# Eight of sixteen row gathers issued two experts ahead, and their two tiles turned inside the choice of width

## The chip, the cores and the metric

One core of a Trainium2 chip runs the kernel. The metric is device time in microseconds (us), the median of several executions. A profile is one further execution, recorded instruction by instruction; its times are counted from the first instruction. PE is the matrix engine (TensorE), DVE is VectorE, ACT is ScalarE, POOL is GpSimd and SP is SyncE, which issues the weight loads.

## The reference

A windowed attention (each query sees the first 8 keys and its last 96) over 4 batches of 8 heads, 768 positions and 64 dimensions makes 3072 rows x of 512 numbers. A router then sends each row to one of 8 experts:

```python
xn = x / (norm(x) + 1e-6);  en = expert_emb / (norm(expert_emb) + 1e-6)
logits = xn @ en.T / tau
expert_idx = argmax(logits, axis=1);  gate_w = softmax(logits)[expert_idx]
for e in range(8):
    mask = expert_idx == e
    h = maximum(x[mask] @ w1[e], 0)                      # 512 -> 1024
    out[mask] = gate_w[mask, None] * (h @ w2[e])         # 1024 -> 512
```

## The kernel before

The first 190 us are the attention and the routing; they leave x in DRAM (`x_dram`) and, for each expert, the list of its rows. From then on a Python loop, unrolled, treats experts 0 to 7 one after another. The change is in that loop, from expert 1 on. All engines run their instructions in the order in which the program lists them.

**PE, for expert e.** First comes the *choice of width*: a switch with nine arms, one for each count of rows from 256 to 512 in steps of 32. In the chosen arm `first_by_seven` (L1331) makes the hidden values with seven products instead of eight, sixteen matmuls each (L1347). After a product DVE adds what it left in PSUM to an earlier one (L1357), and the fourth product can write its bank only when DVE has read the second product out of it. The arm then makes the second matrix product for rows beyond 256 (L1281, L1294). Behind the switch stands the *pair* (class `Pair`, L1153 to L1227), the seven products for the first 256 rows. Its last product writes a bank that ACT reads first (L1206), and ACT gets to that only behind an instruction that needs a sum made by DVE (u3, L1189).

**DVE, for expert e.** In the arm: the additions, and at fixed places (`spare`, a list with one entry per place; the first place, ahead of the first product, is empty) the sums of weights. Behind the switch, for e of 2 and more: it ends the pair of expert e-1, then turns the four tiles of gathered rows of expert e+1 (`turn_squares`, L1036 to L1042, four `STREAM_TRANSPOSE`s at L1039), then adds the pair's u2, then makes four sums of the turned rows (L1090 to L1093), then u3.

**POOL, for expert e** (called *stage e* below). `prepare(e + 1)` issues the sixteen gathers of expert e+1 (`gather_quarters`, L1030): four tiles of 128 rows, each in four quarters of 64 KB. From the fifth gather on, before every second one, a small copy (L1029) reads a value that an earlier gather brought, so POOL waits there until the two gathers issued four and three places earlier have landed. Then come the six scatters of finished rows (L1300), and a `drain` (L1795). POOL then goes on to stage e+1. For expert 2 the loop issues four gathers in `prepare` and twelve behind the scatters.

**SP.** The weights of expert e+1 (w1 2 MB, then w2 2 MB) are loaded in place of those of expert e-1: w1 when expert e-1's pair has begun, w2 when it has ended.

The gathered tiles come from a pool of eight buffers, two experts' worth. x after turning has two buffers.

Of the kernel before, what the change touches and what calls it, by code (L numbers as in the profile page):

```python
# [9 lines left out]
F32 = mybir.dt.float32  # L10
# [10 lines left out]
P = 128  # L21
NEG = 1e9
CAP = 512
# [998 lines left out]
def gather_quarters(k, ids, xgs, lo, hi):  # L1022

    src = k.x_dram[:, :].rearrange("t (b c) -> (t b) c", b=4)
    for i in range(lo, hi):
        j, g = divmod(i, 4)
        if g % 2 == 0 and i - lo > 3:
            m, h = divmod(i - 4, 4)
            k.nc.gpsimd.tensor_copy(out=k.landed[0:1, 0:2], in_=xgs[m][0:1, h * P : (h + 2) * P : P])  # L1029
        k.nc.gpsimd.indirect_dma_start(  # L1030
            out=xgs[j][:, g * P : (g + 1) * P], out_offset=None, in_=src,
            in_offset=bass.IndirectOffsetOnAxis(ap=ids[:, j, g : g + 1], axis=0),
        )


def turn_squares(k, xgs, xT, j):  # L1036

    half = P // 2
    k.nc.vector.transpose(  # L1039
        out=xT[:, :, :, j * half : (j + 1) * half].rearrange("p c a (g i) -> p g c a i", i=LACE),  # L1040
        in_=xgs[j][:].rearrange("p (g r c) -> p g c r", g=4, r=SQ),
    )  # L1042
# [345 lines left out]
def expert(k, now, coming, widths, unfinished):  # L1388
# [15 lines left out]
    more, ahead, turns = [], [], []  # L1404
    if coming:
        coming.token_sums, more = token_sums(k, coming.xT)
        if now.e:
            coming.first_sums, ahead = first_sums(k, coming.w[0])
            turns = [lambda j=j: turn_squares(k, coming.rows[2], coming.xT, j) for j in range(CAP // P)]
    spare = [[], spare[:2], spare[2:3], spare[3:], ahead[:1], ahead[1:2]]  # L1410
    tiles = range(2 if now.e else 1, CAP // P)
    ps = None if now.e else k.work0.tile([P, k.DM], F32, name="work", tag="work")
    k.order = list(range(4, 8)) + list(range(4)) if now.e else list(range(8))
# [24 lines left out]
    def choose_next():  # L1438
        if coming:
            give_hint(k, coming.e, widths[coming.e])  # L1440

    out = [scatters]
    if now.e:
        pair = Pair(k, now.rows, a, left, w2, now.sums, not coming)
        choose_next()
        out += unfinished.pop()()
        number = [lambda: widths.append(take_width(k, now.e + 2))] if now.e + 2 < k.E else []
        if now.e == k.E - 2:
            number.append(lambda: load_flag(k))
        if now.e == 2:  # L1450
            ahead.append(lambda: flag_leftover(k))
        if now.e > 1:
            for make in turns:
                make()
        pair.begin(spare=(more, number, ahead[2:]) if now.e > 1 else ([], number, turns + more + ahead[2:]))
        ps = k.work0.tile([P, k.DM], F32, name="work", tag="work")
        unfinished.append(pair.end(ps[:, 0:256]))
        out.append(pair.scatter(1))
    else:
        choose_next()  # L1460
        widths.append(take_width(k, 2))
        out += unfinished.pop()()
        for make in more:
            make()
        second(k, ps, hT, w2, range(k.NF // 2, k.NF))
        unfinished.append(lambda: end_second(k, now.rows, ps))
# [83 lines left out]
def take_width(k, e):  # L1550

    t = Net()
    n = len(widths_of(e))
    engines = ARMS if e else ARMS[:2]
    v = k.nc.values_load(k.pick[0:1, e : e + 1], engines=engines, min_val=0, max_val=n - 1)
    t.index, t.hint = {eng: v for eng in engines}, "expert%d" % e
    return t
# [22 lines left out]
def load_flag(k):  # L1580
    k.any = k.nc.values_load(k.fi[0:1, 1:2], min_val=0, max_val=1)
# [58 lines left out]
def kernel(  # L1640
# [13 lines left out]
    n = Net()  # L1654
# [26 lines left out]
    with ExitStack() as moe:  # L1681
# [40 lines left out]
        def cast(lo, hi):  # L1722
            nc.vector.tensor_copy(out=n.ids[:, lo:hi], in_=n.mt[:, lo:hi, :, 0:2])

        def prepare(e):
            t = Net()
            t.e = e
            t.y, t.y_part = ys[e % 2]
            if e < 2:
                xgs, t.gathers = gather_rows(n, n.ids[:, e], n.xgp)  # L1730
            else:
                xgs = [n.xgp.tile([P, n.DM], F32, name="xg", tag="xg") for _ in range(CAP // P)]
                gather_quarters(n, n.squares[:, e], xgs, 0, 4 if e == 2 else 16)
            t.rows = n.mt[:, e], n.ids[:, e], xgs
            if e < 2:
                t.w = n.w[e]
            else:
                t.w = new_weights(n, (wp_a, n.wp_b)[e % 2])
            return t

        with tc.manual_schedule(engines=ORDERED | set(ARMS) | {mybir.EngineType.Pool}):
# [38 lines left out]
            for e in range(n.E):  # L1780
                now, coming = coming, None
                parts_of(n, now)
                now.width = widths[e]
                if e == 1:
                    now.first_sums = first
                if e + 1 < n.E:
                    coming = prepare(e + 1)
                for scatter in pending:
                    scatter()
                if e == 1:  # L1790
                    gather_quarters(n, n.squares[:, 2], coming.rows[2], 4, 16)
                if e and coming:
                    wait_for(n, load_weights(n, e + 1, coming.w), [n.outs[-1] if e == 1 else n.out_again])

                nc.gpsimd.drain()  # L1795
                pending = expert(n, now, coming, widths, unfinished)
# [33 lines left out]
```

## Time and profile before

| | |
|---|---|
| median of 3 executions | 515.23 us (513.41 to 517.9) |
| the profiled execution | 510.97 us |
| its span, first to last instruction | 509.2 us |
| mean granted clock of TensorE | 0.999 |
| busy: PE, DVE, ACT, POOL | 95%, 64%, 36%, 48% of the span |

The span leaves 1.8 us of the profiled execution outside it. A busy share is an average over the attention and the experts. "Idle before" in a row is the time that the engine did nothing before that instruction, and the name after the arrow is what ended it; "issue" means that the profile shows nothing it waited for.

### The profile page before, as it was taken

How to read it: one execution, taken by the hardware profiler on the slowest of the kernel's cores; microseconds unless marked ns; L12 is line 12 of the kernel's file. 1: busy time of each engine (PE TensorE's matmuls, PEld its weight loads, DVE VectorE, ACT ScalarE, POOL GpSimd, SP SyncE). 2: the span in 40 equal slices, each digit the busy share in tenths (PEclk: the TensorE clock that was granted, in tenths of full speed). 3: DMA queues.
4: the chain of work that ended last, by engine and by line, in shares of the span. 5: the costliest groups of instructions: out<-in, count | busy, mean ns of one | idle time of the engine just before them, and what ended most of it. 6: DMA issues, size and time to landing. Idle time of an engine off the chain costs nothing.

```text
span 509.2 us, 13692 instructions
## 1 busy us (share of the span) xinstructions
PE 484.6 (95%) x5510; PEld 399.1 (78%) x5510; DVE 325.3 (64%) x642; ACT 183.2 (36%) x445; POOL 243.7 (48%) x275
## 2 busy tenths in 40 slices
PE   7999999999999898999899999999979989999995
PEld 7677787787877687879788479789869679859964
DVE  5656677666777665848467745777656764744631
ACT  4967767858665311302112121222112111312210
POOL 4221131251453426477568575826855856854022
PEclk9999999999999999999999999999999999999999
DMA  9989999998542627529661156265354274112001
GB/s 169 195 187 189 216 240 221 201 222 208 159 106 70 180 48 179 180 79 343 203 200 41 53 200 202 75 223 181 108 188 173 54 258 163 43 70 81 0 23 68
DMA packets 112864, 76.35 MB, mean 150 GB/s; under 512 B 88517, under 2 KB 96709, under 8 KB 112721
## 3 DMA queue, kind: packets, MB, share of 16 engines
q1 hardware_dynamic: 103057, 59.00, 44.3%
q0 software_dynamic: 8064, 15.27, 9.6%
q8 instruction: 63, 1.03, 0.9%
q14 instruction: 80, 0.66, 0.4%
q10 hardware_dynamic: 1600, 0.39, 0.3%
HBM read 61.66 MB, written 17.16 MB: 155 GB/s over the span
## 4 chain that ended last, share of the span: by engine, by line
PE 71%; issue 8%; DMA 6%; POOL 6%; DVE 5%; ACT 4%; POOLq 0%; DVEq 0%; ACTq 0%
PE big L1347 22%; PE big L1153 9%; PE od L514 7%; PE work L1281 7%; PE pa L485 5%; PE pa L460 3%; DMA xg<-x_dram,squares 3%; PE work L1153 3%; PE od L524 3%; PE pa L683 2%; POOL out_dram L1300 2%; ACT ex L491 2%; PE big L1324 2%; POOL xg L1030 2%; PE work L1294 1%
## 5 line engine op out<-in xcount | busy, mean ns | idle before, releaser
L1030 POOL DMA_INDIRECT xg<-x_dram,squares x96 | 105.0, 1093 | 57.2 <-issue 42.6
L498 DVE TENSOR_TENSOR ex<-ex,table 126x768 f32<-126x768 f32 x64 | 60.7, 953 | 37.0 <-ACT ex L491 36.8
L1357 DVE TENSOR_TENSOR hT<-big,hT 128x320 f32<-128x320 f32 (+4 forms) x70 | 39.4, 565 | 56.3 <-PE big L1347 55.8
L1347 PE MATMUL big<-xT,w1t 128*128 128x160 f32 (+4 forms) x336 | 59.4, 330 | 1.6 <-issue 1.6
L491 ACT ACTIVATE ex<-pa 126x384 f32<-126x384 f32 (+1 forms) x128 | 53.2, 479 | 16.6 <-PE pa L485 15.8
L1347 PEld LDWEIGHTS big<-xT,w1t 128*128 128x128 f32 x336 | 54.8, 190 | 4.5 <-issue 2.5
L261 POOL DMA_INDIRECT meta<-mt,slot x24 | 28.5, 1187 | 41.3 <-DVE rd L558 18.2
L514 PE MATMUL od<-ex,v 126*64 126x192 f32 (+1 forms) x576 | 46.0, 305 | 0.0
L1359 ACT ACTIVATE hT<-hT 128x320 f32<-128x320 f32 (+4 forms) x42 | 22.3, 531 | 56.6 <-DVE hT L1357 56.6
L514 PEld LDWEIGHTS od<-ex,v 126*64 126x64 f32 x576 | 34.7, 136 | 7.5 <-issue 3.7
L435 POOL COPY v<-v 30x896 f32<-30x896 f32 (+1 forms) x15 | 17.2, 1158 | 47.8 <-DMA v<-in_v_dram 31.5
L1347 PE MATMUL big<-xsum,fsum 128*128 128x160 f32 (+4 forms) x224 | 39.6, 330 | 0.0
L485 PE MATMUL pa<-qT,kT 64*32 64x128 f32 (+3 forms) x2048 | 37.6, 263 | 0.3 <-DVE xs L596 0.2
L485 PEld LDWEIGHTS pa<-qT,kT 64*32 64x32 f32 (+1 forms) x2048 | 29.3, 105 | 10.8 <-issue 6.8
L1347 PEld LDWEIGHTS big<-xsum,fsum 128*128 128x128 f32 x224 | 36.4, 190 | 1.6 <-DVE fsum L1117 0.4
L1300 POOL DMA_INDIRECT out_dram<-y_arm,tids x17 | 18.8, 1106 | 36.1 <-ACT y_arm L1283 26.1
L1281 PE MATMUL work<-w2t,hT 128*128 128x512 f32 x80 | 35.1, 594 | 0.0
L1153 PE MATMUL big<-wsum,hsum 128*128 128x256 f32 x136 | 31.2, 380 | 0.5 <-DVE hsum L1117 0.4
L1153 PEld LDWEIGHTS big<-wsum,hsum 128*128 128x128 f32 x136 | 25.7, 190 | 5.1 <-issue 0.9
L1153 PE MATMUL big<-w2t,hT 128*128 128x256 f32 x112 | 27.8, 386 | 1.9 <-DVE hsum L1118 1.7
L1281 PEld LDWEIGHTS work<-w2t,hT 128*128 128x128 f32 x80 | 15.1, 190 | 17.7 <-issue 17.6
L1153 PEld LDWEIGHTS big<-w2t,hT 128*128 128x128 f32 x112 | 20.6, 190 | 9.0 <-issue 5.4
(250 smaller groups left out, 878.9 us busy)
## 6 DMA issues: line engine op xcount, KB each, us to landing
w1t<-in_moe_w_dram SPq DMA_DIRECT2D x24, 512.0 KB
w2t<-in_moe_w_dram SPq DMA_DIRECT2D x6, 2048.0 KB
v<-in_v_dram SPq DMA_DIRECT2D x32, 192.0 KB
x_dram<-xs SPq DMA_DIRECT2D x23, 256.0 KB
k<-in_k_dram SPq DMA_DIRECT2D x28, 192.0 KB
q<-in_q_dram SPq DMA_DIRECT2D x28, 192.0 KB
w1t<-in_moe_w_dram SPq DMA_DIRECT2D x32, 128.0 KB
w2t<-in_moe_w_dram SPq DMA_DIRECT2D x32, 128.0 KB
```

The costliest lines, as they stand in the source:

```text
L261: i = nc.gpsimd.indirect_dma_start(out=k.meta[:], out_offset=bass.IndirectOffsetOnAxis(ap=slot[:, t : t + 1], axis=0), in_=mt[:, t, :], in ...
L485: i = nc.tensor.matmul(u.sp[e][k0:k1, a * n + c0 : a * n + c1], lhsT=t.kT[rows, j, k0:k1], rhs=t.qT[rows, j * BLK + c0 : j * BLK + c1], st ...
L491: nc.scalar.activation(u.ex[:, e], u.sp[e][0:ROWS, 0 : 2 * u.n].rearrange("p (a c) -> p a c", a=2), AF.Exp, scale=k.scale)
L498: nc.vector.tensor_tensor(out=exv, in0=exv, in1=tab[:, :, 0 : u.n // BLK, :], op=ALU.mult)
L514: nc.tensor.matmul(g.od[a][e * D : (e + 1) * D, at : at + c1 - c0], lhsT=g.v[0:ROWS, 2 * a + e, u.j, :], rhs=u.ex[:, e, a, c0:c1], start=f ...
L1030: k.nc.gpsimd.indirect_dma_start(out=xgs[j][:, g * P : (g + 1) * P], out_offset=None, in_=src, in_offset=bass.IndirectOffsetOnAxis(ap=ids[ ...
L1153: i = self.k.nc.tensor.matmul(ps, lhsT=x[:, f, :], rhs=w[:, f, :], start=f == 0 and not add, stop=True, skip_group_check=True)
L1281: nc.tensor.matmul(ps[:], lhsT=hT[:, f, j * P : (j + 1) * P], rhs=w2[:, f, :], start=i == 0, stop=i == k.NF - 1)
L1300: i = k.nc.gpsimd.indirect_dma_start(out=k.out.rearrange("t (i m) -> (t i) m", i=n), out_offset=bass.IndirectOffsetOnAxis(ap=ids, axis=0), ...
L1347: nc.tensor.matmul(to[f // 2][:, f % 2 * 256 : f % 2 * 256 + h], lhsT=x[:, l, f * P : (f + 1) * P], rhs=y[:, l, 0:h], start=not (add or f ...
L1357: nc.vector.tensor_tensor(out=to, in0=x, in1=z, op=ALU.add)
L1359: nc.scalar.activation(to, to, AF.Relu)
```

## The change

From stage 1 to stage 5 POOL issues the first eight gathers (two tiles) of expert e+2 behind the six scatters and ahead of the drain. `prepare` issues only the other eight, from expert 3 on. On DVE, for e of 2 and more, the first two of the four turns move from behind the switch to the first place inside each arm.

```diff
-    spare = [[], spare[:2], spare[2:3], spare[3:], ahead[:1], ahead[1:2]]
+    early = turns[:2] if now.e > 1 else []
+    spare = [early, spare[:2], spare[2:3], spare[3:], ahead[:1], ahead[1:2]]
...
         if now.e > 1:
-            for make in turns:
+            for make in turns[2:]:
                 make()
...
+        opened = {}
+
+        def rows_of(e):
+            if e not in opened:
+                opened[e] = [n.xgp.tile([P, n.DM], F32, name="xg", tag="xg") for _ in range(CAP // P)]
+            return opened[e]
+
...
-                xgs = [n.xgp.tile([P, n.DM], F32, name="xg", tag="xg") for _ in range(CAP // P)]
-                gather_quarters(n, n.squares[:, e], xgs, 0, 4 if e == 2 else 16)
+                xgs = rows_of(e)
+                gather_quarters(n, n.squares[:, e], xgs, *((0, 4) if e == 2 else (8, 16)))
...
                     gather_quarters(n, n.squares[:, 2], coming.rows[2], 4, 16)
+                if 0 < e < n.E - 2:
+                    gather_quarters(n, n.squares[:, e + 2], rows_of(e + 2), 0, 8)
```

## Rows read from the trace of the kernel before

**Rows 1.** PE's waits from 200 us to the end, summed: who waited, for what, us in total, times, the longest.

```profile
PE work L1153 <- ACT ptmp L1206: 4.8, 2, 3.7
PE big L1347 <- issue: 1.6, 1, 1.6
```

**Rows 2.** PE's timeline around experts 3 to 6: start, us, operation, idle before. The rows at 307.60, 340.55, 378.96 and 418.15 open the arms of experts 3, 4, 5 and 6, that at 342.94 is the second product of an arm, that at 362.84 opens the pair of expert 4, those at 338.72 and 377.13 are the last products of the pairs of experts 3 and 4, and that at 371.57 is the last but one.

```profile
307.60 2.34 PE L1347 MATMUL big<-xT,w1t 128*128 128x160 f32 x16
...
338.72 1.99 PE L1153 MATMUL work<-w2t,hsum 128*128 128x256 f32 x8 [1.13 <-ACT ptmp L1206]
340.55 2.55 PE L1347 MATMUL big<-xT,w1t 128*128 128x176 f32 x16
342.94 2.55 PE L1347 MATMUL big<-xsum,fsum 128*128 128x176 f32 x16
...
362.84 1.99 PE L1153 MATMUL big<-w2t,hT 128*128 128x256 f32 x8
...
371.57 1.89 PE L1153 MATMUL big<-w2t,hT 128*128 128x256 f32 x8
377.13 1.99 PE L1153 MATMUL work<-w2t,hsum 128*128 128x256 f32 x8 [3.67 <-ACT ptmp L1206]
378.96 2.76 PE L1347 MATMUL big<-xT,w1t 128*128 128x192 f32 x16
...
418.15 3.48 PE L1347 MATMUL big<-xT,w1t 128*128 128x240 f32 x16 [1.64 <-issue]
```

**Rows 3.** DVE's timeline behind the switch of expert 3 (first three rows) and of expert 4 (last three): the turns, u2, u3; the turns up to the late one, the late one, u3.

```profile
330.30 4.05 DVE L1039 STREAM_TRANSPOSE xT<-xg 128x512 f32<-128x512 f32 x4
334.25 0.40 DVE L1158 TENSOR_TENSOR ptmp<-big,ptmp 128x256 f32<-128x256 f32 x1
...
337.35 0.41 DVE L1158 TENSOR_TENSOR ptmp<-big,ptmp 128x256 f32<-128x256 f32 x1
...
365.13 3.06 DVE L1039 STREAM_TRANSPOSE xT<-xg 128x512 f32<-128x512 f32 x3
371.66 1.10 DVE L1039 STREAM_TRANSPOSE xT<-xg 128x512 f32<-128x512 f32 x1 [3.47 <-DMA xg<-x_dram,squares]
...
375.76 0.42 DVE L1158 TENSOR_TENSOR ptmp<-big,ptmp 128x256 f32<-128x256 f32 x1
```

**Rows 4.** The chain of work that ended last, at the late tile: start, us, what.

```profile
365.83 5.71 DMA xg<-x_dram,squares
```

**Rows 5.** DVE's timeline, its first addition in the arms of experts 2 to 6.

```profile
266.55 1.29 DVE L1357 TENSOR_TENSOR hT<-big,hT 128x512 f32<-128x512 f32 x2 [4.47 <-PE big L1347]
...
311.12 0.49 DVE L1357 TENSOR_TENSOR hT<-big,hT 128x320 f32<-128x320 f32 x1 [3.83 <-PE big L1347]
...
344.40 0.52 DVE L1357 TENSOR_TENSOR hT<-big,hT 128x352 f32<-128x352 f32 x1 [2.85 <-PE big L1347]
...
383.13 0.56 DVE L1357 TENSOR_TENSOR hT<-big,hT 128x384 f32<-128x384 f32 x1 [3.14 <-PE big L1347]
...
423.36 0.66 DVE L1357 TENSOR_TENSOR hT<-big,hT 128x480 f32<-128x480 f32 x1 [7.49 <-PE big L1347]
```

**Rows 6.** POOL's timeline: the last gather of stage 1, the first gathers of stages 2 and 3, the last scatter of stage 3, the first and last gather and the first scatter of stage 4, the first gather of stage 5 and its first guarding copy.

```profile
245.77 0.95 POOL L1030 DMA_INDIRECT xg<-x_dram,squares  x1 [0.30 <-issue]
250.29 0.94 POOL L1030 DMA_INDIRECT xg<-x_dram,squares  x1 [3.57 <-PE big L1153]
...
293.14 0.99 POOL L1030 DMA_INDIRECT xg<-x_dram,squares  x1 [4.95 <-issue]
...
331.01 0.98 POOL L1300 DMA_INDIRECT out_dram<-y,idss  x1 [0.30 <-issue]
340.76 1.31 POOL L1030 DMA_INDIRECT xg<-x_dram,squares  x1 [8.77 <-issue]
...
365.83 0.95 POOL L1030 DMA_INDIRECT xg<-x_dram,squares  x1 [0.30 <-issue]
367.08 1.02 POOL L1300 DMA_INDIRECT out_dram<-y_arm,tids  x1 [0.30 <-issue]
...
378.15 1.08 POOL L1030 DMA_INDIRECT xg<-x_dram,squares  x1 [3.61 <-issue]
...
387.77 0.17 POOL L1029 COPY landed<-xg 1x2 f32<-1x2 f32 x1 [4.75 <-DMA xg<-x_dram,squares]
```

**Rows 7.** Gathers from issue to landing, least, median and greatest: those issued from 340 to 346 us (first row), and those from 388 to 406 us (second row).

```profile
DMA to landing us min/median/max: 6.0/6.2/6.5
...
DMA to landing us min/median/max: 2.5/2.6/3.3
```

**Rows 8.** SP's timeline, the load of w2 at the beginning of arm 4.

```profile
340.74 0.38 SPq L170 DMA_DIRECT2D w2t<-in_moe_w_dram  x1
```

**Rows 9.** The drain of stage 3: count, ns, start.

```profile
L1795 POOLq DRAIN  x1: 18532/18532/18532, 321.3 to 321.3; - x1
```

**Rows 10.** PE's branch into the arm of expert 6: count, ns, start.

```profile
L1825 PEldq COMPARE_BRANCH  x1: 3980/3980/3980, 413.9 to 413.9; - x1
```

**Rows 11.** A sum on DVE and a gather on POOL that lie side by side.

```profile
357.90 1.21 DVE L1116 TENSOR_TENSOR w1t<-w1t 128x1024 f32<-128x1024 f32 x1
...
358.04 1.93 POOL L1030 DMA_INDIRECT xg<-x_dram,squares  x1 [0.16 <-issue]
```

## Prediction

> **What bounds the kernel now.** I began with PE's waits [rows 1], since PE is busy 95% of the span. Among the experts little is left to gain there: 4.8 us in two waits for ACT's L1206, and 1.6 us that the profile gives no releaser for. PE's timeline [rows 2] places them: 1.13 us ahead of the last product of expert 3's pair, 3.67 us at the same place for expert 4, and 1.64 us ahead of arm 6. The reader is to see in [rows 2] that the arms of the other experts follow on without a gap, so that any gain has to come out of these 6.4 us.
>
> DVE's timeline [rows 3] says why ACT was late. In expert 3 the four turns take from 330.30 to 334.25, u2 follows, the four sums follow, and u3 comes at 337.35. Nothing is late in landing there; DVE simply has too much between the end of the switch and u3. In expert 4 three turns go through and the fourth waits 3.47 us for a gather. The chain [rows 4] names it: issued at 365.83, landed 5.71 us later. So the second wait is POOL's. POOL's timeline [rows 6] shows that POOL never rests: stages 2, 3, 4 and 5 begin at 250.29, 293.14, 340.76 and 378.15, so that they take 42.9, 47.6 and 37.4 us. PE, from arm to arm without its waits [rows 2], needs 31.8 us for expert 3 (340.55 - 307.60 - 1.13), 34.7 for expert 4 and 37.6 for expert 5. POOL is as slow as PE or slower there.
>
> **The change, part by part.**
>
> **Two turns leave the stretch behind the switch**, for experts 2 to 6. Four took 4.05 us up to u2's start at 334.25, that is 3.95 us, so two are worth 2.0 us [rows 3]. In expert 3 that is more than the 1.13 us that PE waits: all of it goes. Next in line is then the last product but one, which PE would end anyway.
>
> **The last eight gathers of an expert come first in their stage**, not last. For expert 4 the sixteenth gather began 25.1 us after the stage did (365.83 - 340.76 [rows 6]). As one of eight it would begin about 12 us after it, and land some 3 to 6 us later [rows 7]; DVE asks for it some 25 us after the arm began (365.13 [rows 3] against 340.55 [rows 2]). The stage may lag the arm by 7 us and the tile is still in time. The 3.67 us go, and what is late next is nothing in this stretch: u3 would be done at about 370.6 (365.13 + 2.0 + the 3.1 us from u2's start to u3's in expert 3 + its own 0.4), ACT needs another us, and PE asks for the result at 373.3, one product after 371.57 [rows 2].
>
> **The two turns in the arm** cost DVE 2.05 us at its beginning. DVE stood idle there for 4.47, 3.83, 2.85, 3.14 and 7.49 us ahead of its first addition [rows 5], so that they cost nothing if their eight gathers have landed. If not, DVE waits in the arm, and the additions queue behind it. PE feels it at the fourth product, three products after the arm's beginning: 3 x 2.39 = 7.2 us in arm 4 (342.94 - 340.55 [rows 2]) and 3 x 2.6 = 7.8 us in arm 5. With 0.5 us for the addition and 1.05 for the second turn ahead of it, the eighth gather must land within 5.6 us of the beginning of arm 4 and within 6.2 us of that of arm 5. That is the new wait, and it lies on PE's path from that point on.
>
> **POOL's count** is the same: 22 gathers and scatters in a full stage, four guarding copies instead of six. But eight gathers move to a stage earlier, past the drain and ahead of the next stage's others. Stage 1 grows by eight gathers, half of the 26 us that sixteen took in stage 4 (340.76 to 366.78, the end of the last [rows 6]): 13 us. Stage 2 so begins at 263 instead of 250.29, or at 267 if the landings are slowed by the weight loads as in [rows 7]. Of the stages that follow, the trace has 42.9, 47.6 and 37.4 us, none with the gathers in this order. The 47.6 holds 8.77 us behind the last scatter [rows 6], which were the drain [rows 9]: it ended at 339.8. I take 40 us for stages 2 and 3, between the shortest and stage 2's own, and 37.4 for stage 4. The bounds are 37.4 and the times as traced. Stage 4 then begins at 343 to 347 and stage 5 at 380 to 384, and the early gathers have landed about 1.5 us before that, since only the drain and a branch stand between.
>
> Against the limits: PE without its first wait begins arm 4 at 339.4, so that the eighth gather is wanted by 345.0 and lands at 341.5 to 345.5: 0 to 0.5 us of waiting. Arm 5 begins at 374.1 or a little later, the gather is wanted by 380.3 and lands at 379 to 383: 0 to 2.7 us. In arm 2 the first addition comes at 266.55 [rows 5], so that a landing up to 265.5 costs nothing; in arm 3, by the same count, POOL has 7 us in hand; arm 6 has the longest products and follows the 1.64 us that stay. I count nothing for these three. I take the middle, **1.4 us given back**.
>
> **What stays.** The 1.64 us ahead of arm 6 are PE's branch of 3.98 us [rows 10]. PE's instructions don't change; I count nothing, with 1.6 us either way as bounds, since what the branch waits for isn't shown.
>
> **Two rules weighed.** Where DVE adds 1024 numbers from two operands, a gather beside it takes 1.93 us instead of 0.95 [rows 11, 6]; beside the turns of expert 4 (365.13 on) the gather at 365.83 took 0.95 and the scatter at 367.08 took 1.02 [rows 3, 6]. So turns don't hold POOL up. The Trainium skill, "SBUF — State Buffer", section "SBUF: two separate sides", says that some DVE operations hold a port pair that GpSimd needs, for their whole length. By that rule, if turns were of this kind, the two moved ones would stand beside the first gathers of a stage and cost POOL about 2 us each time; the sum would be 2 us smaller for it at arm 5. The trace disagrees for turns, and I go by it.
>
> The landings took 2.6 us in a quiet stretch and 6.2 while w2 was being loaded [rows 7, 8]. The Trainium skill, "DMA: Bandwidth & Descriptors", section "Anatomy of one DMA — SWDGE (gpsimd) path", gives some 2.0 us plus bytes over 436 GB/s, an estimate of 2.15 us for 64 KB. By that no early gather would be late, and the sum would keep its 1.4 us. The rows differ, and they decide.
>
> **The sum** for the profiled execution: 510.97 - 1.13 - 3.67 + 1.4 = 507.6 us, 3.4 us less. The median of the runs shown lies 4.3 us over the profiled execution, and where those us go is not in the trace; carried over, the change gives 515.23 - 3.4 = **511.8 us**.
>
> **The rivals.**
>
> *More is gained* (22 in 100). Executions without the profile took 2.4 to 6.9 us more than the profiled one, a wide spread for a kernel whose PE work is fixed. If these are further waits of the kind at 371.66, for gathers that come last in a stage that is itself late, the change removes most of them: 515.23 - 4.8 - 1 to 4 = 506.5 to 509.5. For it: before, the last landing has no slack. Against it: a slow POOL also delays the early gathers.
>
> *POOL takes it back* (25 in 100). The waits at arms 4 and 5 come to 3 to 6 us, since stage 3 keeps most of its 47.6 us. Stage 4 then begins at 350 and the gather lands 3.5 us too late for arm 4. 513.5 to 517. The same time comes out if the early gathers aren't early: the scatters ahead of them can't be issued before expert e-1's pair has ended.
>
> *Slower* (8 in 100). Stages 2 and 3 keep 42.9 and 47.6 us: 267 + 90.5 = 357.5 for stage 4, the gather lands at 356, eleven us past the limit of 345. PE gets 11 us later at arm 4, less 4.8: 515.23 + 6 = 521. It decides from the point at which stage 4 begins later than 351.5, where 5 us are lost.
>
> **How the numbers follow.** The forecast's own range is 510 to 513.5 and it has 45 in 100. A measurement of this kernel tells little under 1%, which is 5.2 us: 510.1 and 520.4 are the marks. Faster by more: the 22 of the first rival, and 10 of the forecast's 45 for its lower end and the branch: 0.32. Slower by more: most of the last rival, 0.07. The rest, 0.61, lies within 1%. The range of 8 in 10 leaves out the lower part of the first rival and the last one: 507 to 517.5.
>
> **What would show it.** In the profile after, PE's two waits for L1206 should be gone, and behind the switch DVE should show two turns with no wait for a gather. At the beginning of each arm from expert 2 on there should be two turns, and the test is what stands ahead of the second in arms 4 and 5: a wait of DVE for the gather, followed by one of PE for L1357 or for the bank. On POOL, stages 2 to 5 should begin at about 265, 305, 345 and 382. The prediction is wrong if stage 3 stays near 47 us, if the branches of PE move, or if the unexplained 4.3 us shrink or grow with the change.

## The result, and the profile after

Over 20 executions each the changed kernel takes 513.94 us (median; 509.78 to 521.52) and the kernel before 514.12 us (508.72 to 521.89). The ratio of changed to before is 1.0055, interval [1.0030, 1.0079]; it leaves disturbed executions out, so it is not the ratio of the two medians. The forecast was 3.4 us less; nothing was gained, and the ratio's interval leaves out 1 on the slower side. The profiled execution of the changed kernel takes 514.13 us (span 512.3, mean granted clock 0.993) against 510.97.

PE's waits from 200 us to the end, in the columns of [rows 1]:

```profile
PE big L1347 <- DVE hT L1357: 4.0, 2, 2.4
PE big L1153 <- DVE hsum L1118: 1.2, 1, 1.2
PE big L1347 <- issue: 1.1, 1, 1.1
```

The 4.8 us for L1206 of [rows 1] are gone. In their place PE waits 4.0 us for DVE's additions in the arms. PE's timeline places them; the rows at 261.61, 380.12 and 421.45 open arms 2, 5 and 6, the other two are fourth products:

```profile
261.61 3.62 PE L1347 MATMUL big<-xT,w1t 128*128 128x256 f32 x16
...
274.04 3.72 PE L1347 MATMUL big<-xsum,fsum 128*128 128x256 f32 x16 [1.62 <-DVE hT L1357]
...
380.12 2.76 PE L1347 MATMUL big<-xT,w1t 128*128 128x192 f32 x16
...
390.46 2.87 PE L1347 MATMUL big<-xsum,fsum 128*128 128x192 f32 x16 [2.38 <-DVE hT L1357]
...
421.45 3.48 PE L1347 MATMUL big<-xT,w1t 128*128 128x240 f32 x16 [1.14 <-issue]
```

DVE's timeline: arm 2 (two rows), the stretch behind the switch of experts 3 and 4 (turns and u3 of each), arm 5 (three rows):

```profile
271.35 2.06 DVE L1039 STREAM_TRANSPOSE xT<-xg 128x512 f32<-128x512 f32 x2 [4.55 <-issue]
273.33 1.24 DVE L1357 TENSOR_TENSOR hT<-big,hT 128x512 f32<-128x512 f32 x2
...
337.20 2.08 DVE L1039 STREAM_TRANSPOSE xT<-xg 128x512 f32<-128x512 f32 x2
...
342.27 0.42 DVE L1158 TENSOR_TENSOR ptmp<-big,ptmp 128x256 f32<-128x256 f32 x1
...
369.99 2.09 DVE L1039 STREAM_TRANSPOSE xT<-xg 128x512 f32<-128x512 f32 x2
...
375.07 0.42 DVE L1158 TENSOR_TENSOR ptmp<-big,ptmp 128x256 f32<-128x256 f32 x1
...
381.16 1.10 DVE L1039 STREAM_TRANSPOSE xT<-xg 128x512 f32<-128x512 f32 x1 [1.89 <-issue]
388.89 1.08 DVE L1039 STREAM_TRANSPOSE xT<-xg 128x512 f32<-128x512 f32 x1 [6.62 <-DMA xg<-x_dram,squares]
389.89 0.98 DVE L1357 TENSOR_TENSOR hT<-big,hT 128x384 f32<-128x384 f32 x2
```

Behind the switch all is as intended: two turns, no wait for a gather, u3 5.1 us after the turns began instead of 7.1 and 10.6 [rows 3]. In arm 5 the second turn waits 6.62 us for a gather. In arm 2 nothing is waited for, and yet the first turn begins 9.7 us after PE opened the arm. POOL's timeline, the last early gather of stage 4 and the first gather of stage 5:

```profile
382.66 0.94 POOL L1030 DMA_INDIRECT xg<-x_dram,squares  x1 [0.30 <-issue]
390.43 0.94 POOL L1030 DMA_INDIRECT xg<-x_dram,squares  x1 [6.82 <-issue]
```

From the opening of arm 2 to that of arm 7 the profiled execution before takes 208.96 us and that after 207.56 us: 1.4 us less. From arm 7 to PE's end both take 37.5 us. The loss lies ahead of arm 2, which opens at 261.61 instead of 256.91, and there the change touches nothing that PE does. PE's timeline at one matmul of the attention, in the changed kernel (first row) and in the kernel before:

```profile
146.11 0.40 PE L219 MATMUL pa<-oh,prefix 128*128 128x24 f32 x2 [2.45 <-ACT ex L491]
...
142.87 0.40 PE L219 MATMUL pa<-oh,prefix 128*128 128x24 f32 x2 [0.56 <-ACT ex L491]
```

The windows view of the 6.8 us that begin 0.5 us behind its start (stretch, length; busy us and count of PE, PEld, DVE, ACT, POOL; granted clock; DMA share, GB/s), again of the changed kernel:

```profile
146.60:153.40 6.80, 6.80 (x94) 5.09 (x95) 3.81 (x11) 3.05 (x8) 3.41 (x3) 0.50 0.47 82
```

and the same window of the kernel before:

```profile
146.60:153.40 6.80, 6.30 (x147) 4.84 (x147) 4.48 (x16) 3.30 (x10) 3.79 (x4) 1.00 0.42 83
```

After a wait of 2.45 us TensorE ran at half its clock (the 1.2 GHz level) for 6.8 us: 94 matmuls instead of 147. That is 3.4 us of work at full clock. The changed kernel was 1.35 us behind just ahead of this matmul, 1.07 of them lost in one wait of PE at 34.59 us for which the profile gives no releaser. The longer wait and the half clock made that 6.4 us; 1.7 us came back up to arm 2, in waits that are longer in the kernel before. The experiments show whether this belongs to the change.

### The profile page after: what moved, and what is told of

The parts are those of the page before. It is cut to its first block, busy times and chain, and to the rows that moved or that the text cites. A ratio compares the mean times of both kernels' runs of the same rounds, so it can differ in the third digit from the quotient of the medians.

```text
span 512.3 us, 13673 instructions
## 1 busy us (share of the span) xinstructions
PE 487.2 (95%) x5510; PEld 401.1 (78%) x5510; DVE 325.9 (64%) x642; ACT 183.9 (36%) x445; POOL 235.6 (46%) x265
## 4 chain that ended last, share of the span: by engine, by line
PE 51%; DVE 6%; issue 5%; DMA 5%; POOL 3%; ACT 1%; POOLq 0%; SPq 0%; DVEq 0%; ACTq 0%
PE big L1347 21%; PE big L1153 10%; PE work L1281 7%; PE work L1153 3%; PE pa L683 2%; DMA xg<-x_dram,squares 2%; PE work L1294 2%; POOL out_dram L1300 2%; PE big L1324 2%; PE work L1072 1%; DMA xg<-x_dram,idss 1%; POOL xg L1030 1%; PE od L514 1%; DMA w1t<-in_moe_w_dram 1%; DVE xT L1039 1%
## 5 line engine op out<-in xcount | busy, mean ns | idle before, releaser
L1030 POOL DMA_INDIRECT xg<-x_dram,squares x96 | 102.5, 1068 | 61.1 <-issue 43.7
L1357 DVE TENSOR_TENSOR hT<-big,hT 128x320 f32<-128x320 f32 (+4 forms) x70 | 38.7, 560 | 26.4 <-PE big L1347 26.0
L514 PE MATMUL od<-ex,v 126*64 126x192 f32 (+1 forms) x576 | 47.9, 313 | 0.0
L261 POOL DMA_INDIRECT meta<-mt,slot x24 | 26.9, 1121 | 43.2 <-DVE xs L596 13.1
L1039 DVE STREAM_TRANSPOSE xT<-xg 128x512 f32<-128x512 f32 x24 | 25.1, 1080 | 27.5 <-DMA xg<-x_dram,squares 14.1
L1300 POOL DMA_INDIRECT out_dram<-y_arm,tids x17 | 20.5, 1204 | 38.8 <-ACT y_arm L1283 33.1
```

Source lines behind the costliest of these rows:

```text
L261: i = nc.gpsimd.indirect_dma_start(out=k.meta[:], out_offset=bass.IndirectOffsetOnAxis(ap=slot[:, t : t + 1], axis=0), in_=mt[:, t, :], in ...
L514: nc.tensor.matmul(g.od[a][e * D : (e + 1) * D, at : at + c1 - c0], lhsT=g.v[0:ROWS, 2 * a + e, u.j, :], rhs=u.ex[:, e, a, c0:c1], start=f ...
L1030: k.nc.gpsimd.indirect_dma_start(out=xgs[j][:, g * P : (g + 1) * P], out_offset=None, in_=src, in_offset=bass.IndirectOffsetOnAxis(ap=ids[ ...
L1039: k.nc.vector.transpose(out=xT[:, :, :, j * half : (j + 1) * half].rearrange("p c a (g i) -> p g c a i", i=LACE), in_=xgs[j][:].rearrange( ...
L1300: i = k.nc.gpsimd.indirect_dma_start(out=k.out.rearrange("t (i m) -> (t i) m", i=n), out_offset=bass.IndirectOffsetOnAxis(ap=ids, axis=0), ...
L1357: nc.vector.tensor_tensor(out=to, in0=x, in1=z, op=ALU.add)
```

## The experiments

On one chip, that of the second and the fifth group below, the kernel before takes about as long as in the result. On the two chips of the other groups it takes 526 to 537 us, and there it is mostly single waits that are compared.

**First group.** `before_again` and `after_again` are the two kernels unchanged. `gathers_alone` keeps the early gathers and puts all four turns back behind the switch; `turns_later` keeps the gathers and moves the two turns to the second place of the arm, behind the additions that the second product needs.

The edit of `gathers_alone`:

```diff
-    early = turns[:2] if now.e > 1 else []
-    spare = [early, spare[:2], spare[2:3], spare[3:], ahead[:1], ahead[1:2]]
+    spare = [[], spare[:2], spare[2:3], spare[3:], ahead[:1], ahead[1:2]]
...
-            for make in turns[2:]:
+            for make in turns:
```

and of `turns_later`:

```diff
-    spare = [early, spare[:2], spare[2:3], spare[3:], ahead[:1], ahead[1:2]]
+    spare = [[], spare[:2] + early, spare[2:3], spare[3:], ahead[:1], ahead[1:2]]
```

> The kernel before, once more, for its stretch of experts and the stretch ahead of them apart. The stretch of experts, from PE's first product of arm 2 to that of arm 7, took 208.96 us in the first trace of before and 207.56 in that of after. My theory, that the change acts among the experts alone: 208 to 211 us here, with PE's waits for L1206 in the pairs of experts 3 and 4, while the stretch ahead of arm 2 (256.91 us in before, 261.61 in after) moves by some us from execution to execution, with a granted clock of 0.98 to 1.0. The rival, that the changed program is slower ahead of the experts too: 256 to 258 us ahead of arm 2 here, and about 261 in the copy of after.

> The changed kernel, once more. My theory: 206.5 to 208.5 us for the stretch of experts, no wait for L1206, but PE waits for DVE's addition of 1.6 us in arm 2 and of 1 to 3 us in arm 5; ahead of arm 2 the same spread as in before, 256 to 262. The rival: 260 us or more ahead of arm 2 whenever it runs.

> The early gathers alone: all four turns stand behind the switch again. My theory (DVE enters an arm about 3 us after its branch, 5.6 in arm 2, so that two turns have no cover there, and the eighth gather is late in arm 5): the 1.6 and 2.4 us at arms 2 and 5 go, the 1.1 us ahead of the last product of expert 3's pair come back, the 3.7 us of expert 4 stay away. Stretch of experts 204.5 to 206 us. The rival, that early gathers crowd POOL so that the eight gathers issued in the stage itself come too late for the stretch behind the switch: PE's wait for L1206 in expert 4 or 5 is 2 us or more, and 207 to 210.

> The change with its two early turns one place later in the arm: behind the second product's additions and two sums of weights instead of ahead of the first product. My theory: the late gather of arm 5 has 5 us more and DVE's entry into the arm is out of the way, so that both waits in arms 2 and 5 go and none for L1206 comes back: 203.5 to 205 us for the stretch of experts, about 4 us less than before, and 1% less in time. The rival, that DVE is full behind the second product: waits for additions of 0.5 to 1.5 us in arms 3 and 4 instead, 205.5 to 208.

Measured: 531.37, 536.96, 533.2 and 533.82 us, where the runs of the kernel before beside them take 525.85 us. The kernel before differs from itself by a ratio of 1.0081 [1.0012, 1.0150], so that interval doesn't hold all that makes two runs of one program differ, and the ratio of the changed kernel, 1.0195 [1.0131, 1.0259], can't be put down to the change alone. The stretches from arm 2 to arm 7 take 212.7, 223.1, 221.9 and 230.2 us, all four longer than expected, so every expected total is missed. The waits in arm 2 are clear. PE's timeline of `after_again` and of `turns_later` at the fourth product of arm 2:

```profile
275.53 3.72 PE L1347 MATMUL big<-xsum,fsum 128*128 128x256 f32 x16 [1.69 <-DVE hT L1357]
```

```profile
277.75 2.54 PE L1347 MATMUL big<-xsum,fsum 128*128 128x256 f32 x11
```

Arm 2's wait comes again in the copy and is absent with the turns later. But `turns_later` has waits elsewhere that its expectation had ruled out. PE's timeline at the fourth product of arm 3 and at the last product of expert 4's pair:

```profile
326.00 2.44 PE L1347 MATMUL big<-xsum,fsum 128*128 128x160 f32 x16 [1.20 <-DVE hT L1357]
...
398.35 3.78 PE L1153 MATMUL work<-w2t,hsum 128*128 128x256 f32 x8 [12.08 <-ACT ptmp L1206]
```

In that arm DVE entered only 5.9 us after its branch. Ahead of the second wait ACT stood idle for 8.26 us until an event that the profile only calls remote; what that was is open.

In `gathers_alone` PE waits 7.2 us in four waits for L1206, and at expert 4 no gather is late any more, the four turns following each other:

```profile
374.11 4.04 DVE L1039 STREAM_TRANSPOSE xT<-xg 128x512 f32<-128x512 f32 x4
```

So the order of the gathers removes the late landing of [rows 4]. At the end of expert 4's pair PE still waited 3.94 us, where ACT itself had waited 3.33 us for something without a name; in `gathers_second` (third group) that pair ends without a wait. Expert 3's pair ends with a wait of 1.50 us in both.

**Second group**, on the chip where the kernel before takes 512.73 us (median of 31). `after_third` is the changed kernel, `later_second` is `turns_later`, `w2_held` is the changed kernel in which the load of w2 for expert e+1 waits for the eight early gathers of that expert, and `later_and_held` is `turns_later` with the same hold. The hold adds three lines, so that L1357 is L1360 there.

```diff
-def load_weights(k, e, w):
+def load_weights(k, e, w, behind=()):
...
-    nc.sync.dma_start(w[1][:], k.w2[e].rearrange("(f p) m -> p f m", p=P))
+    last = nc.sync.dma_start(w[1][:], k.w2[e].rearrange("(f p) m -> p f m", p=P))
+    wait_for(k, last, behind)
...
-                    gather_quarters(n, n.squares[:, e + 2], rows_of(e + 2), 0, 8)
+                    early[e + 2] = gather_quarters(n, n.squares[:, e + 2], rows_of(e + 2), 0, 8)
...
-                    wait_for(n, load_weights(n, e + 1, coming.w), [n.outs[-1] if e == 1 else n.out_again])
+                    wait_for(n, load_weights(n, e + 1, coming.w, early.get(e + 1, [])), [n.outs[-1] if e == 1 else n.out_again])
```

> The changed kernel once more. Theory (VectorE reaches its first addition only some 3 us, in arm 2 5.6 us, after its branch, so the two turns ahead of it are not covered; and an early gather that lands late beside w2's load holds the second turn of arm 5): the fourth product of arm 2 waits 1.5 to 1.8 us for hT of VectorE (1.62 in the first profile), that of arm 5 between 0 and 3 us depending on the landing; no wait for the ScalarE copy of line 1206 over 1.5 us. Stretch from arm 2 to arm 7: 206 to 209 us where no wait without a releaser falls in it. Rival (the waits of the first profile were accidents of one execution): arm 2 without this wait.

> The two turns stand at the second place of the arm, behind the first product's additions, not ahead of them. Theory: neither arm 2's wait (1.62 us) nor arm 5's (2.38 us) is there, and the waits for the ScalarE copy of line 1206 (4.8 us before) stay away: the stretch from arm 2 to arm 7 is 203.5 to 205.5 us where no wait without a releaser falls in it, 2 to 4 us less than in the changed kernel. Rival (VectorE has no room behind the first product either): the wait moves to the next product, 0.8 to 2.2 us in an arm, and the stretch is 206 us or more.

> The changed kernel with the load of w2 for the next expert held until the eight early gathers of that expert have landed. Theory (the late landing comes from the w2 load beside it): in arm 5 the last early gather lands some 2.6 us after its issue and not 6.2, the wait of arm 5 (2.38 us) falls under 0.5 us, and arm 2's wait of 1.6 us stays, since no gather stands ahead of it. Stretch from arm 2 to arm 7: 204.5 to 206.5 us without a wait that has no releaser. Rival (GpSimd's stage issues it late, whatever the load does): arm 5's wait stays at 1 us or more, and the issue stands over 2 us behind the arm's beginning.

> Both: the two turns at the second place of the arm, and the load of w2 held until the eight early gathers have landed. Theory: no wait at the fourth products, none for line 1206's copy; stretch from arm 2 to arm 7 203.5 to 205 us, at most 0.5 us beside the kernel with the turns later alone. Rival (the held load comes late): waits of TensorE for w2 in the second halves of the arms, each over 0.5 us.

Measured: 515.0 us and 1.0055 [1.0007, 1.0103]; 513.01 us and 1.0022 [0.9981, 1.0063]; 513.03 us and 0.9973 [0.9915, 1.0031]; 509.55 us and 0.9963 [0.9917, 1.0009]. The starts and waits of the profiled executions on this chip, with those of the first pair and of the fifth group (us, read from PE's timelines; half clock is the length of the stretches at granted clock 0.50):

| kernel | arm 2 opens | half clock ahead of it | arm 2 to arm 7 | half clock in it | waits in it |
|---|---|---|---|---|---|
| before | 256.9 | 0 | 208.96 | 0 | pairs 1.1, 3.7; branch 1.6 |
| before_fifth | 257.3 | 3.4 | 212.83 | 6.8 | pairs 1.3, 5.0; branch 1.4 |
| after | 261.6 | 6.8 | 207.56 | 0 | arms 1.6, 2.4; branch 1.1 |
| after_third | 257.9 | 0 | 212.08 | 6.8 | arms 2.1, 2.6; branch 1.3 |
| later_second | 261.3 | 6.8 | 210.27 | 6.8 | arm 5 1.9; pair 1.0; branch 1.9 |
| w2_held | 257.8 | 0 | 210.42 | 6.8 | arms 0.9, 3.0; branch 1.0 |
| later_and_held | 261.5 | 6.8 | 204.87 | 0 | pair 0.9; branch 2.0 |
| held_third | 260.8 | 3.4 | 205.12 | 0 | pair 1.2; branch 2.1 |

`after_third` opens arm 2 at 257.9 us, so the changed kernel need not lose the 4.7 us of the first profile. Over all twenty profiles, half clock ahead of arm 2 stands in four of the five of the kernel before (5.4 us on average) and in ten of the fifteen of the changed kernels (3.9 us): nothing there points to the change. It has both new waits again, and behind each TensorE ran at half clock. PE's timeline at the fourth product of arm 2:

```profile
270.77 5.41 PE L1347 MATMUL big<-xsum,fsum 128*128 128x256 f32 x16 [2.05 <-DVE hT L1357]
```

and the windows view of two stretches, which begin inside the fourth products of arms 2 and 5:

```profile
270.90:274.30 3.40, 3.40 (x9) 2.69 (x10) 2.68 (x3) 0.00 (x0) 2.93 (x4) 0.51 0.19 55
390.40:393.80 3.40, 3.40 (x12) 3.40 (x12) 2.21 (x3) 0.00 (x0) 2.52 (x3) 0.50 0.16 42
```

The product takes 5.41 us instead of 3.72, so that the wait of 2.05 (1.5 to 1.8 were expected) costs another 1.7.

DVE's timeline of `w2_held`, the turns of arm 2 and the second turn of arm 5; then PE's, the fourth product of arm 5; then POOL's, the last early gather of stage 4:

```profile
264.64 2.08 DVE L1042 STREAM_TRANSPOSE xT<-xg 128x512 f32<-128x512 f32 x2 [1.67 <-issue]
...
385.14 1.08 DVE L1042 STREAM_TRANSPOSE xT<-xg 128x512 f32<-128x512 f32 x1 [5.71 <-DMA xg<-x_dram,squares]
```

```profile
386.71 3.57 PE L1350 MATMUL big<-xsum,fsum 128*128 128x192 f32 x10 [3.01 <-DVE hT L1360]
```

```profile
382.58 0.94 POOL L1031 DMA_INDIRECT xg<-x_dram,squares  x1 [0.30 <-issue]
```

SP's timeline, the load of w2 in arm 5 of the changed kernel (first row) and of `w2_held`:

```profile
380.31 0.39 SPq L170 DMA_DIRECT2D w2t<-in_moe_w_dram  x1
...
385.37 0.38 SPq L170 DMA_DIRECT2D w2t<-in_moe_w_dram  x1
```

The rival came true, and of the theory only the landing. The last early gather lands 2.6 us after its issue (382.58 to 385.14) instead of 6.2, now that the load comes behind it. But arm 5 opened at 375.75, so that the issue itself comes 6.8 us into the arm, and the wait stays, with 3.0 us. In the first profile the same sum was 2.5 us for the issue and 6.2 for the landing. And arm 2's wait is gone, which the theory hadn't foreseen: DVE turns 6.8 us after the arm's opening (257.79), not 9.7.

`later_second` keeps a wait of 1.9 us in arm 5, since there too the second turn waited for a late gather (3.97 us), and its stretch misses what was expected, with half clock twice. `later_and_held` is the only one of the four with no wait in an arm, and its 204.87 us lie in the expected 203.5 to 205, though 5.4 us below `later_second` where 0.5 were expected. Waits for the held load, its rival, didn't come. DVE's timeline in arm 2 and arm 5:

```profile
271.89 2.09 DVE L1042 STREAM_TRANSPOSE xT<-xg 128x512 f32<-128x512 f32 x2
...
387.37 1.10 DVE L1042 STREAM_TRANSPOSE xT<-xg 128x512 f32<-128x512 f32 x1
388.77 1.10 DVE L1042 STREAM_TRANSPOSE xT<-xg 128x512 f32<-128x512 f32 x1 [0.30 <-DMA xg<-x_dram,squares]
```

The turns follow the sums with 0.30 us lost in these two arms.

**Third and fourth group**, on two chips where the kernel before takes 536.69 and 532.08 us. `early_first` is the changed kernel with the eight early gathers issued ahead of the stage's scatters instead of behind them (for expert 1 the place is unchanged), `later_first` is `turns_later` with the same; `gathers_second`, `early_second`, `later_ahead` and `held_second` repeat `gathers_alone`, `early_first`, `later_first` and `later_and_held`; `before_third` and `before_fourth` are the kernel before.

```diff
+                if 1 < e < n.E - 2:
+                    gather_quarters(n, n.squares[:, e + 2], rows_of(e + 2), 0, 8)
                 for scatter in pending:
                     scatter()
                 if e == 1:
                     gather_quarters(n, n.squares[:, 2], coming.rows[2], 4, 16)
-                if 0 < e < n.E - 2:
-                    gather_quarters(n, n.squares[:, e + 2], rows_of(e + 2), 0, 8)
+                    gather_quarters(n, n.squares[:, 3], rows_of(3), 0, 8)
```

> The kernel before, unchanged, against itself. Theory: ratio 1.000 within its interval; waits of 1.1 and 3.7 us at the ends of the pairs of experts 3 and 4 come again within 1 us each; the part ahead of arm 2 takes 257 to 258 us without a stretch of half clock in it and 259 to 262 us with one, as in the changed kernels (257.8 to 261.6), so that the 4.7 us there in the first pair of profiles are not the change's. Rival (the change makes the part ahead of arm 2 longer): never over 258 us, and no half clock ahead of arm 2.

> The eight early gathers, with all four turns behind the switch as in the kernel before. Theory: no wait for hT of VectorE at the fourth product of an arm (1.6 to 2.6 us in the changed kernel), and of the waits for line 1206's copy that of expert 4 goes, since no gather comes last there any more, while 1 to 3.5 us of DVE's turns remain in the pairs' ends; stretch from arm 2 to arm 7 206 to 208.5 us where no half clock falls in it. Rival (the gathers themselves, earlier or in two blocks, hold other work back): waits of TensorE that neither kernel has, over 1 us, and a stretch of 209 us or more.

> The changed kernel with the eight early gathers issued ahead of the stage's scatters and not behind them. Theory (arm 5's wait comes from the place of these gathers at the end of GpSimd's stage): they are all issued by the beginning of arm 5, VectorE's second turn there follows the first without a gap (6.6 to 6.8 us before), and arm 5's wait for hT falls from 2.4 to 2.6 us to what VectorE's late entry alone gives, 0 to 1.6 us; arm 2's wait of 1.6 to 2.0 us stays. Rival (transfers beside the loads land late wherever they are issued): arm 5's gap at the second turn stays over 3 us.

> The two turns at the second place of the arm and the early gathers ahead of the scatters. Theory: none of the waits of the change is left (arm 2, arm 5), none for line 1206's copy over 0.5 us; stretch from arm 2 to arm 7 203.5 to 205.5 us, as 204.87 with w2's load held; time 1 to 4 us under the kernel before. Rival (the scatters, now 13 us later, hold the arms' outputs or the next stage back): waits of ScalarE or TensorE at the arms' second halves, and 207 us or more.

> The kernel before, unchanged, against itself, once more. Theory: ratio 1.000 within its interval where the chip takes some 510 us for it; its profile has the waits at the ends of the pairs of experts 3 and 4 (1.1 and 3.7 us), each within 1 us, no wait over 0.5 us at a fourth product; a stretch of half clock ahead of arm 2 in about half of the executions.

> Turns at the second place and w2's load held, once more. Theory: stretch from arm 2 to arm 7 204 to 206 us, no wait over 0.5 us at a fourth product or for line 1206's copy, ratio to the kernel before 0.992 to 0.998. Rival (the 204.87 us were one lucky execution): a stretch of 207 us or more, ratio 1.000 or more.

> Early gathers ahead of the scatters, turns first in the arm, as in early_first. Theory: arm 2's wait of 1.0 to 2.0 us stays, arm 5's (2.4 to 2.6 us in the changed kernel) falls to 0 to 1 us, no gap between the two turns of arm 5; stretch 205 to 207.5 us without half clock in it. Rival: arm 5's wait stays over 1 us.

> Early gathers ahead of the scatters, turns at the second place, as in later_first. Theory: neither arm's wait, stretch 203.5 to 205.5 us, ratio 0.992 to 0.998. Rival (the scatters 13 us later hold something back): waits of ScalarE or TensorE in the arms' second halves, 207 us or more.

Measured, as ratios: 1.0032 [0.9977, 1.0088] for `before_third`, 1.0222 [1.0140, 1.0305] for `gathers_second`, 1.0105 [1.0056, 1.0153] for `later_first` (`early_first` has only its median, 546.46 us); 0.9992 [0.9934, 1.0050] for `before_fourth`, 1.0370 [1.0297, 1.0443] for `held_second`, 1.0162 [1.0057, 1.0266] for `early_second`, 1.0178 [1.0083, 1.0273] for `later_ahead`. Two copies of the kernel before have 1.000 in their intervals, as expected, though of the two pair waits only one of 1.9 us is in `before_fourth`, and `before_third` opens arm 2 at 269.9 us, where 257 to 262 were expected. Every stretch and ratio expected of the variants was missed. Stretches of 207 us and more, the rivals' sign, stand in the kernel before too (221.1 and 222.8 us), so they decide nothing. The waits of the arms can be read. PE's timeline of `early_first`, the fourth products of arms 2 and 5; then DVE's, the turns of arm 5:

```profile
283.75 2.43 PE L1347 MATMUL big<-xsum,fsum 128*128 128x256 f32 x10 [1.05 <-DVE hT L1357]
...
413.77 2.76 PE L1347 MATMUL big<-xsum,fsum 128*128 128x192 f32 x16
```

```profile
406.47 2.10 DVE L1039 STREAM_TRANSPOSE xT<-xg 128x512 f32<-128x512 f32 x2 [1.68 <-DMA xg<-x_dram,squares]
```

With the early gathers ahead of the scatters the two turns of arm 5 follow each other without a gap and PE doesn't wait there, while arm 2's wait stays (1.05, and 1.53 us in `early_second`). DVE's first instruction in arm 5 comes at 406.2 us, so that the 1.68 us are its late entry and not the gather that the row names.

But this doesn't show that the place of the gathers removes the wait. `after_again`, on the chip of `early_second`, has the gathers behind the scatters and no wait in arm 5 either. Its POOL, DVE and PE: the last early gather of stage 4, the turns and the fourth product of arm 5:

```profile
376.35 1.72 POOL L1030 DMA_INDIRECT xg<-x_dram,squares  x1 [0.30 <-issue]
...
399.11 2.12 DVE L1039 STREAM_TRANSPOSE xT<-xg 128x512 f32<-128x512 f32 x2 [1.81 <-DMA out_dram<-y,pids]
...
405.74 2.76 PE L1347 MATMUL big<-xsum,fsum 128*128 128x192 f32 x16
```

That gather is issued 21.6 us ahead of arm 5 (397.94), since PE's path is slower on these chips and POOL gains on it in either order. What the totals there consist of is seen around the opening of expert 4's pair. PE's timeline and a window of `before_fourth`, then both of `held_second`:

```profile
382.94 2.07 PE L1153 MATMUL big<-w2t,hT 128*128 128x256 f32 x4 [6.03 <-issue]
```

```profile
379.50:386.30 6.80, 3.36 (x8) 2.73 (x9) 1.87 (x2) 0.85 (x2) 3.43 (x4) 0.50 0.31 104
```

```profile
385.07 2.04 PE L1156 MATMUL big<-w2t,hT 128*128 128x256 f32 x4 [5.81 <-issue]
```

```profile
378.20:395.30 17.10, 8.71 (x19) 6.14 (x20) 0.41 (x2) 1.21 (x3) 10.20 (x13) 0.50 0.29 81
```

PE stands still for about 6 us for a cause that the profile doesn't name, in the kernel before too, and the half clock around it lasts 6.8 us in one and 17.1 in the other. Over the stretches from arm 2 to arm 7 on these two chips it lasts 0 to 10.2 us in three profiles of the kernel before and 6.8 to 20.5 in nine of the changed kernels, whose ratios, in the six that have one (1.0105 to 1.0370), all lie over those of the copies (1.0081 at most). So there the changed kernels are slower; why half clock lasts longer in them is open, and so is which part of the change brings it.

**Fifth group**, on the chip of the second group. `before_fifth` is the kernel before, `held_third` is `later_and_held`.

> The kernel before against itself. Theory: ratio 1.000 within its interval; where the chip takes some 510 us for it, its profile has waits of 1.1 and 3.7 us (each within 1 us) at the ends of the pairs of experts 3 and 4, and none over 0.5 us at a fourth product; where it takes 525 us and more, a wait of 4 us or more without a releaser near 385 us, with half clock around it, as in five of the profiles there.

> Turns at the second place and w2's load held. Theory: on a chip that takes some 510 us for the kernel before, stretch from arm 2 to arm 7 204 to 206 us where no half clock falls in it, ratio 0.992 to 0.998; on one that takes 525 us and more, ratio 1.005 to 1.04 through half clock near 385 us, where TensorE waits 4 us or more for something without a releaser. Rival (the kernel is faster on either): ratio under 1.000 there too.

Measured: 511.86 us and 0.9948 [0.9904, 0.9992] for the copy, 510.31 us and 0.9967 [0.9928, 1.0006] for `held_third`, beside 514.03 us (23 executions). PE's timeline at the end of expert 4's pair in the copy, then a window around it:

```profile
379.08 3.78 PE L1153 MATMUL work<-w2t,hsum 128*128 128x256 f32 x8 [4.97 <-ACT ptmp L1206]
```

```profile
377.50:384.30 6.80, 5.22 (x14) 4.50 (x15) 3.88 (x6) 1.23 (x3) 4.22 (x5) 0.50 0.18 43
```

The waits of [rows 2] come again (1.3 and 5.0 us, the second 0.3 more than was expected at most), and this time with half clock: the last product takes 3.78 us, not 1.99. `held_third` repeats its stretch, 205.12 us. All executions on this chip together give 513.1 us for the kernel before (64, two of over 1.2 ms left out) and 510.1 for `later_and_held` (22), but an identical copy of the kernel before stands 0.5% from it in the same session, so that I don't call it faster.

## Why the prediction was wrong

**The gain: right.** Both waits for L1206 went as worked out, expert 3's because two turns left the stretch, expert 4's because the late gather comes first. The forecast had 1.13 + 3.67 us, and none of it is left. The moved turns are needed: with the gathers alone waits for L1206 stay (7.2 and 2.9 us in all, 1.5 of them at the end of expert 3's pair in either run). The turns without the early gathers were not run.

**The cover in arm 2: the step that failed.** "DVE stood idle there for 4.47 ... us ahead of its first addition [rows 5], so that they cost nothing if their eight gathers have landed." The row names PE as what ended that idle time, and I read it as time in which DVE could have worked. It wasn't in the arm yet. DVE's branch into arm 2 and its first instruction there, in the kernel before (count, ns, start):

```profile
L1825 DVEq COMPARE_BRANCH  x1: 59/59/59, 260.8 to 260.8; - x1
...
L1415 DVEq BRANCH_PREFETCH_HINT  x1: 45/45/45, 266.4 to 266.4; - x1
```

DVE came into the arm at 266.4 us and added at 266.55. Its branch had been issued at 260.8, so 5.6 us lay between. And the branch itself stood 3.9 us behind PE's opening of the arm (256.91), since DVE was still at the sums of weights behind the switch of expert 1; into arms 3 to 6 it was issued 0.3 to 3.6 us ahead of PE's opening. The limit for arm 2 was to be worked out from there, as for the others: 266.4 + 2.05 for the turns + 0.6 for the addition = 269.05, while PE wants the bank after three products of 3.6 us, at 267.7. That makes 1.3 us; 1.62 were measured. Each of the two parts alone would have been covered: by the same sum 5.6 us from a branch at PE's opening end at 265.2, and in `w2_held` the branch lies 3.9 us behind as well, but 2.7 us of entry leave no wait. The size follows DVE's entry: 5.6 us from branch to first instruction go with 1.62, 6.1 with 2.05 (`after_third`), 5.0 with 1.05 (`early_first`). `turns_later`, beside `after_again` on one chip, shows that the turns at this place are what PE waits for: without them arm 2 has no wait. In the other arms of the kernel before DVE entered after 0.5 to 3.1 us, and there the same sum leaves room; no turn was late there for this reason.

**The landing in arm 5: foreseen, and sized too small.** I took 1.4 us for arms 4 and 5 together, out of 0 to 0.5 and 0 to 2.7; arm 4 had no wait and arm 5 2.38. Stage 4 took 43.4 us (347.00 to 390.43) where I had 37.4, the length of a stage with another order of gathers. Counted from arm 2's opening, stage 5 began 3.7 us later than I took it and arm 5 only 1.3 us. The eighth gather was issued 2.5 us into the arm and landed 6.2 us later beside the load of w2. `w2_held` shows the second half: with the load held the landing takes 2.6 us. That a place ahead of the scatters would mend the first is not shown, since on the chips where it was run the changed kernel has no wait in arm 5 either. The stages 2 to 5 began at 272.9, 306.9, 347.0 and 390.4, against 265, 305, 345 and 382 in an execution whose arm 2 opens 4.7 us later.

**The branch** at arm 6 lost 1.14 us instead of 1.64, within what was bounded.

**The sum of the stretch.** Forecast -3.4. Measured -1.4 in the first profile: 1.62 more in arm 2, 1.0 more in arm 5, 0.5 less at the branch, 0.1 less elsewhere.

**The carrying over to the median: wrong as well.** A wait had one price in my sum, its length. On the chip half clock follows some of the waits, in the kernel before too, and then the price is 1.7 to 3.4 us higher: 208.96 and 212.83 us in two profiles of the kernel before, 207.56 and 212.08 in two of the changed one. The "unexplained 4.3 us" between the profiled execution and the median are probably in part of this kind: the profiled one had a clock of 0.999, and of the 64 executions of the kernel before on the chip of the second group the ten with more than 0.996 take 508.9 us (median), the 25 with 0.987 to 0.992 take 515.3. That the changed kernel loses by half clock more often on the chips of these four profiles is not shown, with two profiles of each. The rest of the +0.55%, which `after_third` has again, over the 1.4 us less of the first pair, stays open; copies of the kernel before differ from it by -0.5 to +0.8%, as much as what is to be explained.

**The rules weighed.** In arm 5 a turn began at 381.16 and the gather beside it, at 381.38, took 0.98 us: turns don't hold POOL up. The Trainium skill, "SBUF — State Buffer", section "SBUF: two separate sides", says that some DVE operations hold a port pair that GpSimd needs; the trace again shows turns not to be of them. The landing of the eighth gather decided arm 5 with 6.2 us. By the Trainium skill, "DMA: Bandwidth & Descriptors", section "Anatomy of one DMA — SWDGE (gpsimd) path", it would have been an estimated 2.15 us; only the landings with no weights being loaded come near that (2.6 in `w2_held` and in the second row of [rows 7]).

## What to carry to other kernels

Idle time ahead of an instruction is cover only from the moment at which the engine can take work: look for its branch and for its first instruction behind it, even one that does no work, and count both from the event at which the other engine opens the stage, before you put anything into the gap. A moved transfer needs its deadline and its producer's end counted from the same event, with the stage's length taken for the new order. And where two copies of one program differ by 0.5%, a gain of 3 us in 514 has to be shown wait by wait.

## What the runs showed that was not expected

DVE took 0.5 to 6.1 us from its branch into an arm to its first instruction there, and the time differs with the build of the program: at expert 2 it was 4.9 to 6.1 us in all sixteen profiles without the hold of w2's load, and 2.7 to 2.9 us in the four with it, in which DVE's own instructions are those of the changed kernel or of `turns_later`. What sets it is not shown. TensorE ran at half clock in stretches of 3.4 and 6.8 us, on the other two chips of up to 17.1, with a wait of PE ahead of them or inside them wherever I looked among the experts, but not behind every wait: not behind the 3.67 us of [rows 2]. Landings of gathers of the same 64 KB took 2.6 or 6.2 us, depending on whether 2 MB of weights were being loaded beside them.
